# A transformer block with modulated norms: the attention gate wholly on VectorE, its first weights loaded earlier

## The chip, the cores and the metric

One core of one Trainium2 chip runs the whole program. The core has a matmul engine (TensorE, called PE in the profile, with its weight loads as PEld), VectorE (DVE), ScalarE (ACT), GpSimd (POOL) and SyncE (SP), which work on their own instruction queues and wait for each other by semaphores. The metric is the time of one execution on the device in microseconds (us); lower is better. Three executions of the kernel before gave 243.42, 243.48 and 243.65 us, median 243.48.

## The reference

A diffusion-transformer block: batch 2, 256 tokens each, width D = 1152, two heads of 576, MLP width 4608, all in bf16. Six vectors per batch row come from `silu(c) @ w_mod`: shift, scale and gate for attention, and the same three for the MLP.

```python
mod = (silu(c) @ w_mod).reshape(B, 6, 1, D)
shift_a, scale_a, gate_a, shift_m, scale_m, gate_m = [mod[:, i] for i in range(6)]
h = layernorm(x) * (1 + scale_a) + shift_a
q, k, v = split(h @ wqkv)
attn = softmax(einsum('bqhd,bkhd->bhqk', q, k) * Dh ** -0.5)
a = einsum('bhqk,bkhd->bqhd', attn, v).reshape(B, N, D) @ wo
x = x + gate_a * a
h2 = layernorm(x) * (1 + scale_m) + shift_m
return x + gate_m * (gelu(h2 @ w_fc1) @ w_fc2)
```

## The kernel before

All 512 tokens are worked on at once, in 128-row tiles. One big tile in SBUF (`arena`, line 551) is cut by hand into regions, and one in PSUM (`psum`) into eight banks of 512 columns; this is why nearly every row of the profile reads `arena<-psum` or `psum<-arena`, and instructions are told apart by line and shape. All matmuls stand on line 693 (helper `mm`) and all transposes by TensorE on line 696 (`tr`); all loads and stores on line 674 (`dma`); plain evictions out of PSUM on line 688 (ScalarE) or 690 (VectorE), both in `copy_on`.

What sets the order of work: the program is recorded as units (lines 184 to 213) and a planner (`schedule`, line 281) orders them. On PE and SP the order is that of the recording. On VectorE, ScalarE and POOL it is the planner's, by its own cost figures and the length of what hangs on a unit; `order_after` (line 206) adds an edge between two units of one engine, with no data behind it. Each engine then runs its list strictly in order, so one waiting instruction holds all that stand behind it on that engine.

The stages that the change touches, in order of PE:

- K's projection, then `sh` (line 943): the shift of attention by `quad_mm` (line 811). Its stationary operand is the two columns of silu(c), so a matmul makes 2 rows; four of them, at column positions 0, 32, 64 and 96 of the array, take a quarter of the columns each. "A quad" below is such a group of four.
- Q's projection, first six of its nine chunks in one loop over nine input blocks (`q_kt0` to `q_kt8`, line 1202), each as soon as its block of Q's weights has come. SP loads these blocks (`ld_wq0` to `ld_wq8`, line 916), then the weights of the first FG columns of the gate (`ld_ga0`, `ld_ga3`, `ld_ga6`, three blocks each, line 947), V's weights, the rest of the modulation's weights (`ld_modr`), and WO.
- Scores and softmax of four pairs (batch, head) in the order (0,0), (1,0), (0,1), (1,1), by `s_and_softmax` (line 989): VectorE takes the maximum (`smax`, line 1001) and its negative (`snb`, 1002), ScalarE the exponentials (`sexp`, 1005), VectorE the reciprocal (`sri`, 1007) and the normalisation (`spn`, 1009).
- V in twelve tiles of 128 tokens x 384 columns (`v_proj`, line 1023), each evicted by ScalarE, with the four `pt_transposes` (line 1011) of the probabilities between them; their evictions `PT_ev` are VectorE's for batch 0 and ScalarE's for batch 1.
- `rows` (line 1037): more quads, on PE, for the columns of the modulation that VectorE does not make: the rest of the attention gate, and shift and scale of the second norm. Two VectorE transposes (`mt_0`, `mt_1`, line 1046) bring the latter into place.
- `attn_gate` (line 1054): VectorE makes the first FG columns of the attention gate by multiply-add of weight rows with silu(c), in float32, 18 instructions (nine blocks x two batch rows), then 32x32-block transposes, reductions and a small chain over 32 partitions (lines 1067 to 1079). POOL stores the result to a scratch tensor in DRAM; SP loads it back spread over all partitions (`ld_g0`, `ld_g1`, line 1230).
- `pv_halves` and `pv` (attention times V), evicted by `OT_ev`; then `wo_tile` (line 1149): output projection, the product with the gate on VectorE (line 1161), the residual on POOL (1162), and the second norm's statistics.

NG counts the gate's groups of 128 columns that VectorE makes; FG = 128 NG.

Of the kernel before, what the change touches and what calls it, by code (L numbers as in the profile page):

```python
# [493 lines left out]
ALU = mybir.AluOpType  # L494
# [14 lines left out]
F0 = 9  # L509
KC = 5  # L510
KG = 6
NG = 7
FG = NG * 128


# [8 lines left out]
def c_dve_psum32(n):  # L524
    return 110.0 + 1.13 * n


def c_dve_psum16(n):
    return 110.0 + 0.57 * n
# [14 lines left out]
def build_kernel(nc, x, c, wqkv, wo, w_mod, w_fc1, w_fc2, out):  # L544
# [5 lines left out]
    with (  # L550
# [69 lines left out]
        ROWS = sb(O_R + 4 * W1 - 5 * 2304, 2304)[:, 0:288 - 32 * NG]  # L620
# [3 lines left out]
        GBA = sb(O_R + FG * 17, 128)[0:32, :]  # L624
        GTA = sb(O_R + FG * 17 + 128, 128)[0:32, :]
# [51 lines left out]
        def dve(cost, fn, reads, writes, name):  # L677
            return S.op("dve", cost, fn, reads=reads, writes=writes, name=name)
# [7 lines left out]
        def copy_on(eng, dst, src, n, psum16, name):  # L686
            if eng == "act":
                act(c_act(n), lambda e: e.activation(out=dst, in_=src, func=ACTF.Copy), [src], [dst], name)  # L688
            else:
                dve(c_dve_psum16(n) if psum16 else c_dve_psum32(n), lambda e: e.tensor_copy(dst, src), [src], [dst], name)  # L690

        def mm(o, l, r, st, sp, **kw):
            S.instr(lambda e: e.matmul(o, lhsT=l, rhs=r, start=st, stop=sp, **kw), reads=[l, r], writes=[o])  # L693
# [218 lines left out]
                hk(kt, b)  # L912
        k_pair((4, 3), 1, 1)
        k_pair((0, 2, 1, 4, 3), 2, 1)
        for kt in range(KT):
            dma(WQ[:, kt, :], wqkv_v[:, kt, 0:D], P * D * 2, "ld_wq%d" % kt, run=2304)
        for kt in range(KC, KT - 2):
            for b in range(2):
                for i in range(4 - b):
                    k_pair((kt,), i, b)  # L920
# [22 lines left out]
        S.unit("pe", KT * 4 * 31.0 + 100.0, "sh")  # L943
        for kt in range(KT):
            quad_mm(0, WSH[:, kt, :], 0, 9, kt)
        for k0 in range(0, KT, 3):
            dma(WMODR[:, k0:k0 + 3, 0:FG], wmod_v[:, k0:k0 + 3, 2 * D:2 * D + FG], 3 * P * FG * 2, "ld_ga%d" % k0, run=FG * 2)
        dma(WV, wqkv_v[:, :, 2 * D:3 * D], D * D * 2, "ld_wv", run=2304)
        for k0 in range(0, KT, 3):
            dma(WMODR[:, k0:k0 + 3, FG:3 * D], wmod_v[:, k0:k0 + 3, 2 * D + FG:5 * D], 3 * P * (3 * D - FG) * 2, "ld_modr%d" % k0)  # L950
# [38 lines left out]
        def s_and_softmax(b, h):  # L989
            idx = b * 2 + h  # L990
            bank = s_bank[(b, h)]
            S.unit("pe", 8 * c_mm(256), "S_%d_%d" % (b, h))
            ch = head_chunks[h]
            for jq in range(2):
                for ci, (gq, gk) in enumerate(ch):
                    q0 = b * 256 + jq * 128
                    mm(ps32(bank, jq * 256, 256), QK[:, gq, q0:q0 + 128], QK[:, gk, b * 256:(b + 1) * 256], False, ci == len(ch) - 1,
                       skip_group_check=True)
            s3 = ps32(bank).rearrange("p (j k) -> p j k", j=2)
            mx, nb, rsum, ri, pp = MX[:, idx, :], NB[:, idx, :], RS[:, idx, :], RI[:, idx, :], PP[idx]  # L1000
            dve(c_dve_psum32(512), lambda e: e.tensor_reduce(out=mx, in_=s3, axis=AX.X, op=ALU.max), [s3], [mx], "smax_%d" % idx)  # L1001
            dve(165, lambda e: e.tensor_scalar(out=nb, in0=mx, scalar1=-SCALE, scalar2=None, op0=ALU.mult), [mx], [nb], "snb_%d" % idx)  # L1002
            for jq in range(2):
                o, i_, bb, aa = pp[:, jq, :], ps32(bank, jq * 256, 256), nb[:, jq:jq + 1], rsum[:, jq:jq + 1]
                act(c_act(256, 1) + 200, lambda e, o=o, i_=i_, bb=bb, aa=aa: e.activation(out=o, in_=i_, func=ACTF.Exp, scale=SCALE, bias=bb, accum_out=aa),  # L1005
                    [i_, bb], [o, aa], "sexp_%d_%d" % (idx, jq))
            dve(165, lambda e: e.reciprocal(out=ri, in_=rsum), [rsum], [ri], "sri_%d" % idx)
            rib = ri.unsqueeze(2).broadcast_to([P, 2, 256])
            dve(c_dve_tt16(512), lambda e: e.tensor_tensor(out=pp, in0=pp, in1=rib, op=ALU.mult), [pp, ri], [pp], "spn_%d" % idx)

        def pt_transposes(b, h):
            idx = b * 2 + h
# [17 lines left out]
            copy_on("act", V[:, t, ci * CH:(ci + 1) * CH], o, CH, False, "v_ev%d_%d" % (t, ci))  # L1030


        row_parts = ((3, NG, 18), (4, 18, 27))

        last_red = [None]

        def rows():
            S.unit("pe", KT * (864 - 32 * NG) / 2.4 + 500.0, "rows")
            for kt in range(KT):
                for bank, g0, g1 in row_parts:  # L1040
                    quad_mm(bank, WMODR[:, kt, :], g0, g1, kt)
            n = 288 - 32 * NG
            copy_on("act", ROWS, ps32(3, 0, n), n, False, "rows_ev")
            for i, (bank, c0) in enumerate(((3, n), (4, 0))):
                src, dst = ps32(bank, c0, 288), MT[:, i * 288:(i + 1) * 288]
                u = dve(c_dve_psum32(288), lambda e, src=src, dst=dst: e.transpose(dst, src), [src], [dst], "mt_%d" % i)
                S.order_after(u, last_red[0])
            sc, so = MT[:, 288:576].rearrange("p (k r) -> p k r", r=32)[:, :, 0:2], SC1M.rearrange("p (k b) -> p k b", b=2)
            dve(170, lambda e: e.tensor_scalar(out=so, in0=sc, scalar1=1.0, scalar2=None, op0=ALU.add), [sc], [so], "sc1m")
            for b in range(2):  # L1050
                dma(scratch[0, b, FG:D].rearrange("(k q c) -> q k c", q=4, c=32), ROWS[b:128:32, :].rearrange("p (k c) -> p k c", c=32),
                    2304 - 2 * FG, "st_g%d" % b, eng="pool")

        def attn_gate():
            for kt in range(KT):
                for b in range(2):
                    o, w, s1 = ACCA[:, b, :], WMODR[:, kt, 0:FG], ST32[:, b * 9 + kt:b * 9 + kt + 1]
                    if kt == 0:
                        dve(150 + FG * 0.6, lambda e, o=o, w=w, s1=s1: e.tensor_scalar(out=o, in0=w, scalar1=s1, scalar2=None, op0=ALU.mult),  # L1059
                            [w, s1], [o], "ga_%d_%d" % (b, kt))  # L1060
                    else:
                        dve(150 + FG * 1.1, lambda e, o=o, w=w, s1=s1: e.scalar_tensor_tensor(out=o, in0=w, scalar=s1, in1=o, op0=ALU.mult, op1=ALU.add),  # L1062
                            [w, s1, o], [o], "ga_%d_%d" % (b, kt))
            pool(100, lambda e: e.memset(GBA, 0.0), [], [GBA], "gba0")
            for b in range(2):
                a_, t_ = ACCA[:, b, :], ACTA[:, b, :]
                dve(150 + FG * 1.1, lambda e, a_=a_, t_=t_: e.transpose(t_, a_), [a_], [t_], "ga_T%d" % b)
                t3, o = t_.rearrange("p (g r) -> p g r", r=32), GPA[:, 0, b, :]
                last_red[0] = dve(150 + FG * 1.1, lambda e, t3=t3, o=o: e.tensor_reduce(out=o, in_=t3, axis=AX.X, op=ALU.add), [t3], [o], "ga_red%d" % b)
# [7 lines left out]
            g0, gb = GPA[0:32, 0, :, :], GBA.rearrange("p (b g) -> p b g", b=2)[:, :, 0:4 * NG]  # L1077
            dve(200, lambda e: e.tensor_copy(gb, g0), [g0], [gb], "ga_bf")
            dve(200, lambda e: e.transpose(GTA, GBA), [GBA], [GTA], "ga_t")
            for b in range(2):  # L1080
                dma(scratch[0, b, 0:FG].rearrange("(g c) -> g c", c=32), GTA[0:4 * NG, 32 * b:32 * b + 32], FG * 2, "st_ga%d" % b, eng="pool")

        def mlp_gate(prev):
            for b in range(2):
# [31 lines left out]
        def pv_halves():  # L1116
            S.unit("pe", 4 * c_mm(256) + 100.0, "PV_halves")
            for b in range(2):
                for kjt in range(2):
                    for h in range(2):  # L1120
# [110 lines left out]
        v_proj(2, 1)  # L1231
        v_proj(2, 2)
        v_proj(3, 0)
        v_proj(3, 1)
        v_proj(3, 2)
# [108 lines left out]
```

## Time and profile before

| what | value |
|---|---|
| median of three executions | 243.48 us (243.42 to 243.65) |
| the profiled execution's own time | 243.42 us |
| its span, first to last instruction | 241.7 us |
| TensorE matmul busy | 235.7 us (98%) |
| VectorE busy | 115.9 us (48%) |
| ScalarE busy | 68.0 us (28%) |
| GpSimd busy | 21.4 us (9%) |
| bytes moved | 51.58 MB, mean 213 GB/s |

Times in the text are counted from the start of the span. Matmuls overlap in the pipeline, so the time of one in the profile is longer than its share of the stream; what a stage costs is read from the distance between starts, or from the busy time of a stretch. A group line tells line, engine, operation, shapes and count, then busy time and mean duration, then the idle time ahead of it and what ended it. A timeline row starts with its start and its length; consecutive alike instructions are merged into one row with a count. A row of stretches gives, after the stretch, its length and each engine's busy time with the number of instructions (PE, PEld, DVE, ACT, POOL), then the granted clock, the DMA share and GB/s.

### The profile page before, as it was taken

How to read it: one execution, taken by the hardware profiler on the slowest of the kernel's cores; microseconds unless marked ns; L12 is line 12 of the kernel's file. 1: busy time of each engine (PE TensorE's matmuls, PEld its weight loads, DVE VectorE, ACT ScalarE, POOL GpSimd, SP SyncE). 2: the span in 40 equal slices, each digit the busy share in tenths (PEclk: the TensorE clock that was granted, in tenths of full speed). 3: DMA queues.
4: the chain of work that ended last, by engine and by line, in shares of the span. 5: the costliest groups of instructions: out<-in, count | busy, mean ns of one | idle time of the engine just before them, and what ended most of it. 6: DMA issues, size and time to landing. Idle time of an engine off the chain costs nothing.

```text
span 241.7 us, 3956 instructions
## 1 busy us (share of the span) xinstructions
PE 235.7 (98%) x1691; PEld 144.3 (60%) x1699; DVE 115.9 (48%) x229; ACT 68.0 (28%) x137; POOL 21.4 (9%) x38
## 2 busy tenths in 40 slices
PE   6899999999999999999999999999999999999995
PEld 2688844466657666898544444444556666566664
DVE  2654358888994589669999500000122111111112
ACT  4940540546324126973322222333000000000000
POOL 1300000000021476300000110000000000000000
DMA  6999999999994999999963499000000000000000
GB/s 220 369 374 391 390 387 386 404 414 407 391 356 124 321 379 391 392 355 394 343 209 86 122 342 376 8 0 3 0 16 19 16 16 16 19 19 27 22 17 16
DMA packets 30427, 51.58 MB, mean 213 GB/s; under 512 B 1611, under 2 KB 16971, under 8 KB 30411
## 3 DMA queue, kind: packets, MB, share of 16 engines
q1 hardware_dynamic: 29888, 50.73, 58.8%
q0 software_dynamic: 352, 0.60, 0.8%
q8 instruction: 13, 0.21, 0.4%
q10 hardware_dynamic: 171, 0.01, 0.0%
q14 instruction: 3, 0.02, 0.0%
HBM read 50.15 MB, written 1.19 MB: 212 GB/s over the span
## 4 chain that ended last, share of the span: by engine, by line
PE 94%; DMA 3%; SPq 1%; issue 0%; DVE 0%
PE psum L693 92%; DMA arena<-in_wqkv_dram 3%; PE psum L696 2%; SPq L674 1%; DVE arena L1286 0%; DVE arena L1287 0%
## 5 line engine op out<-in xcount | busy, mean ns | idle before, releaser
L693 PE MATMUL psum<-arena 128*128 128x384 bf16 (+9 forms) x1602 | 232.4, 313 | 2.8 <-POOL arena L719 1.5
L693 PEld LDWEIGHTS psum<-arena 128*128 128x128 bf16 (+2 forms) x1610 | 139.0, 97 | 92.0 <-issue 3.8
L1286 DVE TENSOR_TENSOR arena<-psum,arena 128x384 f32<-128x384 f32 (+2 forms) x13 | 6.9, 528 | 88.5 <-PE psum L693 88.5
L1196 ACT ACTIVATE arena<-psum 128x512 bf16<-128x512 f32 (+1 forms) x45 | 22.8, 511 | 42.2 <-PE psum L693 42.2
L688 ACT ACTIVATE arena<-psum 128x512 bf16<-128x512 f32 (+7 forms) x35 | 18.4, 550 | 37.5 <-PE psum L693 37.5
L1091 DVE SCALAR_TENSOR_TENSOR arena<-arena 128x1152 f32<-128x1152 bf16 x16 | 21.3, 1409 | 0.0
L1062 DVE SCALAR_TENSOR_TENSOR arena<-arena 128x896 f32<-128x896 bf16 x16 | 17.7, 1145 | 0.0
L1162 POOL TENSOR_TENSOR arena<-arena 128x384 f32<-128x384 f32 x12 | 10.9, 912 | 13.3 <-DVE arena L1161 11.1
L674 POOL DMA_DIRECT2D dit_scratch<-arena x6 | 3.6, 603 | 92.6 <-ACT arena L688 53.1
L741 DVE BATCH_NORM_STATS2 arena<-arena 128x6 f32<-128x384 f32 (+1 forms) x18 | 9.5, 550 | 4.0 <-DMA arena<-in_x_dram 3.9
L690 DVE CAST arena<-psum 128x512 bf16<-128x512 f32 x11 | 7.5, 690 | 7.4 <-PE psum L693 7.4
L1161 DVE TENSOR_TENSOR arena<-psum,arena 128x384 f32<-128x384 f32 x12 | 6.7, 555 | 3.8 <-PE psum L693 3.8
L1167 ACT ACTIVATE arena<-arena 128x1152 bf16<-128x1152 f32 x4 | 5.4, 1344 | 9.8 <-DVE arena L1166 9.8
L696 PE MATMUL psum<-arena 128*128 128x128 bf16 (+1 forms) x89 | 7.1, 219 | 0.4 <-DMA arena<-in_c_dram 0.4
L696 PEld LDWEIGHTS psum<-arena 128*128 128x128 bf16 (+1 forms) x89 | 5.8, 98 | 2.4 <-DMA arena<-in_c_dram 1.3
L1287 DVE TENSOR_TENSOR arena<-arena 128x384 bf16<-128x384 f32 (+2 forms) x13 | 6.9, 528 | 0.5
L1186 ACT ACTIVATE arena<-psum,arena 128x128 bf16<-128x128 bf16 x16 | 6.1, 455 | 3.0 <-PE psum L696 2.2
L1183 DVE TENSOR_SCALAR arena<-psum,arena 128x128 bf16<-128x128 bf16 x20 | 5.5, 336 | 2.9 <-PE psum L696 2.9
L1005 ACT ACTIVATE arena<-psum,arena 128x256 bf16<-128x256 f32 x8 | 3.7, 469 | 0.4 <-DVE arena L1002 0.3
L745 POOL TENSOR_TENSOR arena<-arena 128x1 f32<-128x1 f32 x6 | 3.3, 553 | 4.5 <-DVE arena L744 4.3
L1001 DVE TENSOR_REDUCE arena<-psum 128x2 f32<-128x512 f32 x4 | 2.7, 686 | 0.9 <-PE psum L693 0.9
L1059 DVE TENSOR_SCALAR arena<-arena 128x896 f32<-128x896 bf16 x2 | 1.3, 684 | 3.6 <-DMA arena<-in_w_mod_dram 3.6
(60 smaller groups left out, 54.1 us busy)
## 6 DMA issues: line engine op xcount, KB each, us to landing
arena<-in_w_fc_dram SPq DMA_DIRECT2D x9, 1152.0 KB, 8.1
arena<-in_w_fc_dram SPq DMA_DIRECT2D x4, 2592.0 KB, 17.5
arena<-in_w_mod_dram SPq DMA_DIRECT2D x3, 1920.0 KB, 19.7
arena<-in_wqkv_dram SPq DMA_DIRECT2D x18, 288.0 KB, 10.0
arena<-in_w_mod_dram SPq DMA_DIRECT2D x3, 864.0 KB, 12.6
arena<-in_wqkv_dram SPq DMA_DIRECT2D x1, 2592.0 KB, 16.9
arena<-in_wo_dram SPq DMA_DIRECT2D x1, 2592.0 KB, 26.1
arena<-in_w_mod_dram SPq DMA_DIRECT2D x1, 2592.0 KB, 18.2
```

What stands on the lines that cost most here:

```text
L688: act(c_act(n), lambda e: e.activation(out=dst, in_=src, func=ACTF.Copy), [src], [dst], name)
L690: dve(c_dve_psum16(n) if psum16 else c_dve_psum32(n), lambda e: e.tensor_copy(dst, src), [src], [dst], name)
L693: S.instr(lambda e: e.matmul(o, lhsT=l, rhs=r, start=st, stop=sp, **kw), reads=[l, r], writes=[o])
L696: S.instr(lambda e: e.transpose(o, i_, idn), reads=[i_, idn], writes=[o])
L741: dve(550, lambda e, s=s, o=o: e.bn_stats(out=o, in_=s), [s], [o], "bn_%s_%d" % (tag, ci))
L1062: dve(150 + FG * 1.1, lambda e, o=o, w=w, s1=s1: e.scalar_tensor_tensor(out=o, in0=w, scalar=s1, in1=o, op0=ALU.mult, op1=ALU.add), [w, s1 ...
L1091: u = dve(1300, lambda e, o=o, w=w, s1=s1: e.scalar_tensor_tensor(out=o, in0=w, scalar=s1, in1=o, op0=ALU.mult, op1=ALU.add), [w, s1, o], ...
L1161: dve(550, lambda e, o=o, ga=ga, x1c=x1c: e.tensor_tensor(out=x1c, in0=o, in1=ga, op=ALU.mult), [o, ga], [x1c], "wo_t1_%d_%d" % (t, ci))
L1162: S.op("pool", 930, lambda e, xs=xs, x1c=x1c: e.tensor_tensor(out=x1c, in0=x1c, in1=xs, op=ALU.add), reads=[x1c, xs], writes=[x1c], name=" ...
L1196: act(c_act(ntok), lambda e: e.activation(out=dst, in_=o, func=ACTF.Gelu_apprx_tanh), [o], [dst], "gelu_%d_%d" % (f, tok0))
L1286: dve(c_dve_psum32(w), lambda e, o=o, gm=gm, t1=t1: e.tensor_tensor(out=t1, in0=o, in1=gm, op=ALU.mult), [o, gm], [t1], "fc2_t1_%d_%d" % ( ...
L1287: dve(c_dve_32(w), lambda e, t1=t1, x1c=x1c, ost=ost: e.tensor_tensor(out=ost, in0=t1, in1=x1c, op=ALU.add), [t1, x1c], [ost], "fc2_out_%d ...
```

## The change

VectorE's share of the attention gate grows from seven groups to all nine (896 to 1152 columns), so no gate column is left to `rows`, and its eviction and two scratch stores fall away. The first of the three gate loads is issued right behind Q's second block of weights. The transposes of the probabilities of (0,1) and (1,1) and the unit `rows` stand later in PE's list. `order_after` edges now put one gate multiply-add behind the normalisation of (0,1) and one behind that of (1,1), the two `mt` transposes behind the end of the gate's small chain, and the eviction `OT_ev_4` behind the second `mt`. The gate's result for both batch rows lies in one transposed tile of 72 groups and is stored in two pieces of 64 and 8 rows.

```diff
-NG = 7
+NG = 9
 FG = NG * 128
...
+        def ga_load(k0):
+            dma(WMODR[:, k0:k0 + 3, 0:FG], wmod_v[:, k0:k0 + 3, 2 * D:2 * D + FG], 3 * P * FG * 2, "ld_ga%d" % k0, run=FG * 2)
+
         for kt in range(KT):
             dma(WQ[:, kt, :], wqkv_v[:, kt, 0:D], P * D * 2, "ld_wq%d" % kt, run=2304)
+            if kt == 1:
+                ga_load(0)
...
-        for k0 in range(0, KT, 3):
-            dma(WMODR[:, k0:k0 + 3, 0:FG], wmod_v[:, k0:k0 + 3, 2 * D:2 * D + FG], 3 * P * FG * 2, "ld_ga%d" % k0, run=FG * 2)
+        for k0 in range(3, KT, 3):
+            ga_load(k0)
...
-            dve(c_dve_tt16(512), lambda e: e.tensor_tensor(out=pp, in0=pp, in1=rib, op=ALU.mult), [pp, ri], [pp], "spn_%d" % idx)
+            u = dve(c_dve_tt16(512), lambda e: e.tensor_tensor(out=pp, in0=pp, in1=rib, op=ALU.mult), [pp, ri], [pp], "spn_%d" % idx)
+            if idx % 2 == 1:
+                S.order_after(ga_units[(1, 7) if idx == 1 else (0, 8)], u)
...
-        row_parts = ((3, NG, 18), (4, 18, 27))
+        row_parts = ((3, 9, 18), (4, 18, 27))
...
-            n = 288 - 32 * NG
-            copy_on("act", ROWS, ps32(3, 0, n), n, False, "rows_ev")
-            for i, (bank, c0) in enumerate(((3, n), (4, 0))):
-                src, dst = ps32(bank, c0, 288), MT[:, i * 288:(i + 1) * 288]
+            for i, bank in enumerate((3, 4)):
+                src, dst = ps32(bank, 0, 288), MT[:, i * 288:(i + 1) * 288]
                 u = dve(c_dve_psum32(288), lambda e, src=src, dst=dst: e.transpose(dst, src), [src], [dst], "mt_%d" % i)
                 S.order_after(u, last_red[0])
+                last_mt[0] = u
...
-            for b in range(2):
-                dma(scratch[0, b, FG:D].rearrange("(k q c) -> q k c", q=4, c=32), ROWS[b:128:32, :].rearrange("p (k c) -> p k c", c=32),
-                    2304 - 2 * FG, "st_g%d" % b, eng="pool")
...
-            dve(200, lambda e: e.transpose(GTA, GBA), [GBA], [GTA], "ga_t")
-            for b in range(2):
-                dma(scratch[0, b, 0:FG].rearrange("(g c) -> g c", c=32), GTA[0:4 * NG, 32 * b:32 * b + 32], FG * 2, "st_ga%d" % b, eng="pool")
+            last_red[0] = dve(200, lambda e: e.transpose(GTA, GBA), [GBA], [GTA], "ga_t")
+            lin = scratch[0].rearrange("b (g c) -> (b g) c", c=32)
+            dma(lin[0:64].rearrange("(j p) c -> p j c", j=2), GTA[:, 0:64].rearrange("p (j c) -> p j c", j=2), 4096, "st_ga0", eng="pool")
+            dma(lin[64:72], GTA[0:8, 64:96], 512, "st_ga1", eng="pool")
...
-            copy_on("dve", OT[:, 4, :], ps32(5), 512, False, "OT_ev_4")
+            S.order_after(copy_on("dve", OT[:, 4, :], ps32(5), 512, False, "OT_ev_4"), last_mt[0])
...
         v_proj(1, 1)
+        v_proj(1, 2)
         pt_transposes(0, 1)
-        v_proj(1, 2)
+        v_proj(2, 0)
+        v_proj(2, 1)
         pt_transposes(1, 1)
-        v_proj(2, 0)
+        v_proj(2, 2)
         rows()
...
-        v_proj(2, 1)
-        v_proj(2, 2)
         v_proj(3, 0)
```

More of the change, by code (lines that the diff above doesn't have):

```diff
@@ L619, in build_kernel @@
         XN2 = [sb(O_R + 4 * W1 - (i + 1) * 2304, 2304) for i in range(4)]
-        ROWS = sb(O_R + 4 * W1 - 5 * 2304, 2304)[:, 0:288 - 32 * NG]
         ACCA = sb(O_R, FG * 8, F32).rearrange("p (b d) -> p b d", b=2)
@@ L623, in build_kernel @@
         GPA = sb(O_R + FG * 16, FG, F32).rearrange("p (q b g) -> p q b g", q=4, b=2)
-        GBA = sb(O_R + FG * 17, 128)[0:32, :]
-        GTA = sb(O_R + FG * 17 + 128, 128)[0:32, :]
+        GBA = sb(O_R + FG * 17, 192)[0:32, :]
+        GTA = sb(O_R + FG * 17 + 192, 192)[0:32, :]
         T1 = [sb(O_X + i * 1536, 1536, F32) for i in range(3)]
@@ L689, in copy_on @@
             else:
-                dve(c_dve_psum16(n) if psum16 else c_dve_psum32(n), lambda e: e.tensor_copy(dst, src), [src], [dst], name)
+                return dve(c_dve_psum16(n) if psum16 else c_dve_psum32(n), lambda e: e.tensor_copy(dst, src), [src], [dst], name)
         def mm(o, l, r, st, sp, **kw):
@@ L1030, in v_proj @@
             copy_on("act", V[:, t, ci * CH:(ci + 1) * CH], o, CH, False, "v_ev%d_%d" % (t, ci))
-        row_parts = ((3, NG, 18), (4, 18, 27))
-        last_red = [None]
+        row_parts = ((3, 9, 18), (4, 18, 27))
+        last_red, last_mt, ga_units = [None], [None], {}
         def rows():
@@ L1061, in attn_gate @@
                     else:
-                        dve(150 + FG * 1.1, lambda e, o=o, w=w, s1=s1: e.scalar_tensor_tensor(out=o, in0=w, scalar=s1, in1=o, op0=ALU.mult, op1=ALU.add),
-                            [w, s1, o], [o], "ga_%d_%d" % (b, kt))
+                        ga_units[(b, kt)] = dve(150 + FG * 1.1, lambda e, o=o, w=w, s1=s1: e.scalar_tensor_tensor(out=o, in0=w, scalar=s1, in1=o,
+                                                                                                               op0=ALU.mult, op1=ALU.add),
+                                                [w, s1, o], [o], "ga_%d_%d" % (b, kt))
             pool(100, lambda e: e.memset(GBA, 0.0), [], [GBA], "gba0")
@@ L1068, in attn_gate @@
                 t3, o = t_.rearrange("p (g r) -> p g r", r=32), GPA[:, 0, b, :]
-                last_red[0] = dve(150 + FG * 1.1, lambda e, t3=t3, o=o: e.tensor_reduce(out=o, in_=t3, axis=AX.X, op=ALU.add), [t3], [o], "ga_red%d" % b)
+                dve(150 + FG * 1.1, lambda e, t3=t3, o=o: e.tensor_reduce(out=o, in_=t3, axis=AX.X, op=ALU.add), [t3], [o], "ga_red%d" % b)
             gp = GPA.rearrange("p q b g -> p q (b g)")
@@ L1076, in attn_gate @@
                 dve(200, lambda e, x_=x_, y_=y_: e.tensor_tensor(out=x_, in0=x_, in1=y_, op=ALU.add), [x_, y_], [x_], "ga_add%d" % b_)
-            g0, gb = GPA[0:32, 0, :, :], GBA.rearrange("p (b g) -> p b g", b=2)[:, :, 0:4 * NG]
+            g0, gb = gp[0:32, 0, :], GBA[:, 0:8 * NG]
             dve(200, lambda e: e.tensor_copy(gb, g0), [g0], [gb], "ga_bf")
-            dve(200, lambda e: e.transpose(GTA, GBA), [GBA], [GTA], "ga_t")
-            for b in range(2):
-                dma(scratch[0, b, 0:FG].rearrange("(g c) -> g c", c=32), GTA[0:4 * NG, 32 * b:32 * b + 32], FG * 2, "st_ga%d" % b, eng="pool")
+            last_red[0] = dve(200, lambda e: e.transpose(GTA, GBA), [GBA], [GTA], "ga_t")
+            lin = scratch[0].rearrange("b (g c) -> (b g) c", c=32)
+            dma(lin[0:64].rearrange("(j p) c -> p j c", j=2), GTA[:, 0:64].rearrange("p (j c) -> p j c", j=2), 4096, "st_ga0", eng="pool")
+            dma(lin[64:72], GTA[0:8, 64:96], 512, "st_ga1", eng="pool")
         def mlp_gate(prev):
```

## The prediction

> **What bounds the kernel now.** I read the page first: its span, the engines' shares and the chain that ended last.
>
> ```profile
> span 241.7 us, 3956 instructions
> ...
> PE 235.7 (98%) x1691; PEld 144.3 (60%) x1699; DVE 115.9 (48%) x229; ACT 68.0 (28%) x137; POOL 21.4 (9%) x38
> ...
> PE 94%; DMA 3%; SPq 1%; issue 0%; DVE 0%
> ```
>
> TensorE (PE) is the chain. Busy shares of pipelined matmuls say little, so I looked next at what PE waited for.
>
> ```profile
> PE psum L693 <- POOL arena L719: 1.5, 1, 1.5
> PE psum L693 <- DMA arena<-in_w_mod_dram: 0.6, 2, 0.4
> PE psum L696 <- DMA arena<-in_c_dram: 0.4, 1, 0.4
> PE psum L693 <- DMA arena<-in_wqkv_dram: 0.2, 1, 0.2
> PE psum L693 <- issue: 0.2, 1, 0.2
> ```
>
> Columns: total us, times, longest. All but the last row lie in the first 11 us, ahead of anything the change touches. After that PE never waits for VectorE (DVE), ScalarE or a load. So the edit can gain only by taking matmul time off PE, and lose only by making PE wait where it does not wait now. The next view is busy time by stretch; the first row is the `rows` unit, the second the shift projection, whose 36 matmuls all have 288 columns.
>
> ```profile
> 64.69:67.14 2.45, 2.45 (x73) 1.62 (x72) 2.45 (x4) 0.49 (x1) 0.00 (x0) 1.00 1.05 384
> 28.68:29.79 1.11, 1.11 (x37) 0.78 (x36) 0.00 (x0) 0.38 (x1) 0.00 (x0) 1.00 1.05 392
> ```
>
> (The 73rd and 37th are a neighbour's tail.) The granted clock is 1.00, so rows can be compared. Four column groups run side by side: 36 matmuls in 1.11 us are 9 passes of 0.122 us. For the edit's longer chains I need VectorE's and ScalarE's rows:
>
> ```profile
> 58.28 0.42 DVE L690 COPY arena<-psum 128x512 bf16<-128x512 bf16 x1 [0.74 <-PE psum L696]
> 62.21 2.21 DVE L1062 SCALAR_TENSOR_TENSOR arena<-arena 128x896 f32<-128x896 bf16 x2
> 72.08 0.23 DVE L1079 STREAM_TRANSPOSE arena<-arena 32x64 bf16<-32x64 bf16 x1
> 106.89 1.54 DVE L1088 TENSOR_SCALAR arena<-arena 128x1152 f32<-128x1152 bf16 x2
> 108.34 21.35 DVE L1091 SCALAR_TENSOR_TENSOR arena<-arena 128x1152 f32<-128x1152 bf16 x16
> 129.72 2.58 DVE L1095 STREAM_TRANSPOSE arena<-arena 128x2304 f32<-128x2304 f32 x1
> ```
>
> ```profile
> 58.06 0.49 ACT L688 ACTIVATE arena<-psum 128x384 bf16<-128x384 f32 x1 [0.73 <-PE psum L693]
> 89.31 1.35 ACT L1167 ACTIVATE arena<-arena 128x1152 bf16<-128x1152 f32 x1 [9.78 <-DVE arena L1166]
> ```
>
> The first line is the eviction that frees the first transposed probabilities; the second the last gate instruction kind at 896 columns; the third the end of the gate at 72.31. The three 1152- and 2304-wide rows belong to the MLP gate and are the very shapes the change needs.
>
> **The change part by part.**
>
> *Rows, removed columns.* Each of 9 passes had a 352-column and a 288-column quad; now two of 288. New unit: 18 x 0.122 = 2.20 us against 2.45, a gain of 0.24 us (the same from the 352 part: 2.45 - 1.11 = 1.34, times 64/352). It is on the chain: PE only. The `rows_ev` eviction on ScalarE (0.22) and two scratch stores on POOL go too, off the chain.
>
> *Moves on PE.* The two transposes go behind one more V tile each, the rows behind V (2,2); as many switches between shapes remain. Zero for PE unless a wait appears.
>
> *First weights ahead of Q's third block.* The two blocks ahead of it land at 29.50 and 30.27. The three shift loads of the same size and shape (864 KB) land 2.3 to 2.55 us apart, so the gate load lands near 32.6 and Q's third block at 33.3 to 33.6 instead of 31.0. PE reaches it after 9 + 12 matmuls of 0.216 us from 30.12, at 34.65. Cover left: 1.1 to 1.35 us. SP issues these loads some 10 us before they land, so its own time (0.5 to 1.1 us for the earlier issue) is hidden. Later loads lag by 3 x 192 KB, 1.5 us: V's weights land at 49.3, first used at 51.7. The three rest-of-modulation loads shrink by as much, so from 62.0 on nothing has moved.
>
> *VectorE's gate.* A 1152-wide multiply-add costs 21.35/16 = 1.33 us where 896 cost 1.06; the first pair 1.54 against 1.28; transposes 1.30 against 1.03 and reductions 1.25 against 1.00 (interpolated between the 896 and 2304 rows). Sum: 16 x 0.27 + 0.26 + 0.54 + 0.5 + 0.1 = 5.7 us more. Starting at 33.7 rather than 37.3, eight of the eighteen fit before Q's evictions at 43.7 (end 43.1), and fourteen instead of thirteen before 58.28. From there follow the built order of both engines. ScalarE now has the eviction of V (0,2), 58.06 above, ahead of the third pair of exponentials, which ran at 56.31; they go to 58.5-59.5. VectorE waits for them: reciprocal 59.6, one multiply-add, normalisation to 61.6-61.7. PE wants that transpose at 62.7 (61.23 + one V tile of 1.46): 1.0 us of cover. The fourth pair ends at 61.2, its normalisation at 63.7, PE wants it at 65.84. Two multiply-adds, transposes and reductions lead to 71.35, the eviction of the second transposed probabilities to 71.7 (needed at 74.4), the small chain (1.69 before, 1.80 in the MLP gate at this width) to 73.5, against 72.31. LN2's two bank transposes (0.81) end at 74.2; the attention evictions start at 76.05: 1.85 us of cover. OT_ev_4, now third in that queue, ends near 78.25; its matmul is due at 79.1.
>
> *The gate's way back.* VectorE's end at 73.5, POOL's issue at 73.8, store landing, SP's issue, load landing. These rows tell of it (count, size, us to landing):
>
> ```profile
> dit_scratch<-arena POOLq DMA_DIRECT2D x2, 0.5 KB, 5.8
> dit_scratch<-arena POOLq DMA_DIRECT2D x2, 1.8 KB, 2.9
> arena<-dit_scratch SPq DMA_DIRECT2D x2, 288.0 KB, 4.3
> ```
>
> The store costs between 2.3 (the MLP gate's, same shape) and 5.95 (the slower of the first pair, issued at 68.0 while weight loads ran); the load between 3.5 and 5.2. I take 2.3 and 3.5, since the weight loads ahead drain at 75.5 as before: gate 0 lands at 79.7, at worst 85.0 (nothing in the rows is quicker). First use is at 80.15. Nor does lateness reach PE at once: the fifth output tile needs the first tile's bank at 84.33, less 0.66; and the first LN2 tile ends on ScalarE at 90.66 (89.31 + 1.35), 1.2 us ahead of its transpose at 91.89, after POOL's five additions of 0.87 that can catch up. Both give 83.7 as the last harmless landing. Loads queued on SP behind the gate move by under 1 us; the next needed one lands at 84.8 for a use past 103.
>
> [...] In the trace the slow pair of stores ran while VectorE was working, the quicker pair while it sat idle (72.31 to 75.36), and after the change two LN2 transposes run right behind the gate. [...]
>
> Sum: the profiled execution took 243.42 us (span 241.7, 1.7 around it); 243.42 - 0.24 + 0 = 243.18. The median of the three runs is 0.06 higher. Forecast 243.2.
>
> **The rivals.**
>
> *Gate rows late (slower).* Place: first output-projection tiles. For it: store rows of 5.95, load rows up to 5.2. Against: the loads that slowed them drain by 75.5. With 5.95 + 3.5 the landing is 83.3, still free; with 5.95 + 5.2 it is 85.0, PE loses 1.3: 244.5. It decides from 83.7.
>
> *A probability transpose that waits.* The third's cover is 1.0 us. If VectorE runs one whole multiply-add (1.33) behind my sum, PE loses 0.3: 243.5; two such, 1.7: 244.9. Against: it is worked out from rows on both sides of the wait.
>
> *Q's third block waits.* Cover 1.1 to 1.35 us; only a landing after 34.65 counts. With another slowest 864 KB spacing (2.55) it would come at 35.9: PE loses 1.2, 244.4. Nothing in the view shows loads out of turn.
>
> *The saving is larger.* If the alternation of two widths also cost something at each of 18 switches, the gain could exceed 0.5 us: under 242.9. Against: 2.45 is already 9 x (0.149 + 0.122).
>
> **How the numbers follow.** What tells from no change is about 0.2%, 0.49 us. Forecast (nothing waits) 0.76, by itself 243.0 to 243.5; late gate 0.06; transpose waits 0.07 (half of it over 0.2%); third block 0.04; larger saving 0.07. Slower: 0.06 + 0.035 + 0.04, so 0.14; faster 0.08 with the scatter; same the remaining 0.78. Range 242.9 to 243.9: it takes in the scatter of the runs (0.23) and the small end of the waits.
>
> **What would show it.** Right: rows stretch 2.2 us; PE's waits unchanged after 11 us; VectorE busy near 121.5; third exponentials at 58.5; gate end near 73.5; gate load issued near 76.2. Wrong: any PE wait on VectorE, ScalarE or a load between 34 and 92, or a gap before the third transpose near 62.7 or before the first LN2 transpose at 91.6.

## The result, and the profile after

The changed kernel takes 242.97 us (median of 22 executions, 242.58 to 244.24) against 243.50 us (22 executions, 243.19 to 243.74) for the kernel before, measured beside it: ratio 0.9979, 95% interval 0.9973 to 0.9986. That is 0.53 us faster, and the interval in microseconds is 0.34 to 0.66. The forecast was a gain of 0.24. So the change does a little more than twice what was forecast, and the question of the experiments is where the other 0.3 us came from.

The first profiled execution of the changed kernel (244.24 us) had TensorE's clock at half for about 3 us of K's projection (granted clock 0.55 from 10.80 to 14.20 us), as one profile of another kernel below (e11) had too (mean granted clock 0.993 in both); so the changed kernel is read below in a second profiled execution, of the unaltered program (e1, 243.08 us). First its page: span and engines' busy time.

```profile
span 241.3 us, 3949 instructions
...
PE 236.2 (98%) x1691; PEld 144.5 (60%) x1699; DVE 121.6 (50%) x229; ACT 67.7 (28%) x136; POOL 20.0 (8%) x36
```

VectorE's busy time is 121.6 us, against 115.9 before and 121.5 forecast. Next what PE waited for in e1 (total us, times, longest).

```profile
PE psum L692 <- POOL arena L718: 1.5, 1, 1.5
PE psum L695 <- DMA arena<-in_c_dram: 0.4, 1, 0.4
PE psum L692 <- DMA arena<-in_wqkv_dram: 0.2, 1, 0.2
PE psum L692 <- issue: 0.2, 1, 0.2
```

No row names VectorE, ScalarE or a load of the gate: every cover that the prediction counted on held. Then the stretch of `rows` in e1 (length, then PE, PEld, DVE, ACT and POOL busy with counts, granted clock, DMA share, GB/s).

```profile
67.90:70.12 2.22, 2.22 (x73) 1.62 (x72) 2.22 (x2) 0.49 (x1) 0.00 (x0) 1.00 1.10 352
```

It was 2.45 and is 2.22. From first start to last start it is 2.331 us before and 2.092 in e1, 0.239 less.

K's projection starts at a moment set by the first loads and differs from execution to execution (10.91 us before, 11.18 in e1), so I compare stretches that begin behind it. From the first transposes of the probabilities (57.86 us in before, 58.14 in e1) to the first matmul of 80 columns (237.42 and 237.46, in the last output tile), PE takes 179.559 us before and 179.320 us in e1: 0.239 less. This is "PE's stretch" below. (Begun in K's projection already, at the five transposes at 15.46 and 15.74 us, the difference is 0.242.) PE gained just what `rows` lost, and nothing was given back. That leaves the stretch behind PE's last matmuls. SyncE's last instructions, before (count, then least, median and longest duration in ns, and first and last start in us):

```profile
L553 SPq COMPARE_BRANCH  x1: 32/32/32, 240.9 to 240.9; - x1
L553 SPq DRAIN  x1: 65/65/65, 241.4 to 241.4; - x1
L553 SPq EVENT_SEMAPHORE  x1: 17/17/17, 241.6 to 241.6; - x1
```

and in e1:

```profile
L553 SPq COMPARE_BRANCH  x1: 33/33/33, 241.0 to 241.0; - x1
L553 SPq DRAIN  x1: 7/7/7, 241.1 to 241.1; - x1
L553 SPq EVENT_SEMAPHORE  x1: 17/17/17, 241.3 to 241.3; - x1
```

Both kernels do the same here: SyncE has waited for the last store, branches out of its list, drains, and ends with a semaphore instruction. From the end of the branch to the start of the drain the trace has 0.410 us before and 0.106 in e1; from the start of the branch to the end of the span 0.715 and 0.353. (Between PE's 80-column matmuls and the branch nothing changed: 3.531 and 3.535 us.) So 0.36 us went out of the last microsecond, far from everything that the change touches on PE and VectorE. The first profiled execution of the changed kernel, with its halved clock ahead, has the same two numbers: PE's stretch 179.320, branch to end 0.357. 0.24 and 0.36 make 0.60, inside the interval of 0.34 to 0.66.

What differs on SyncE is its number of instructions. From its first load to the closing branch it has 77 before and 75 after: two semaphore waits at 75.7 and 76.2 us are gone, those of the gate loads for the two scratch stores of `rows` that the change removed. Of before, by line:

```profile
L471 SPq EVENT_SEMAPHORE  x2: 17/17/17, 75.7 to 76.2; - x2
```

### The profile page after: what moved, and what is told of

Read it like the earlier page. It is cut to its first block, busy times and chain, and to the rows that moved or that the text cites. A ratio compares the mean times of both kernels' runs of the same rounds, so it can differ in the third digit from the quotient of the medians.

```text
span 242.5 us, 3957 instructions
## 1 busy us (share of the span) xinstructions
PE 237.3 (98%) x1699; PEld 145.4 (60%) x1699; DVE 121.5 (50%) x229; ACT 67.8 (28%) x136; POOL 19.9 (8%) x36
## 4 chain that ended last, share of the span: by engine, by line
PE 95%; DMA 3%; SPq 1%; DVE 0%; issue 0%
PE psum L692 93%; DMA arena<-in_wqkv_dram 3%; PE psum L695 2%; SPq L673 1%; DVE arena L1290 0%; DVE arena L1291 0%
## 5 line engine op out<-in xcount | busy, mean ns | idle before, releaser
L692 PE MATMUL psum<-arena 128*128 128x384 bf16 (+8 forms) x1610 | 234.0, 314 | 2.4 <-POOL arena L718 1.5
L687 ACT ACTIVATE arena<-psum 128x512 bf16<-128x512 f32 (+6 forms) x34 | 18.2, 560 | 37.9 <-PE psum L692 37.9
L1064 DVE SCALAR_TENSOR_TENSOR arena<-arena 128x1152 f32<-128x1152 bf16 x16 | 21.9, 1408 | 0.0
L1095 DVE SCALAR_TENSOR_TENSOR arena<-arena 128x1152 f32<-128x1152 bf16 x16 | 21.4, 1414 | 0.0
L673 POOL DMA_DIRECT2D dit_scratch<-arena x4 | 2.4, 609 | 96.6 <-DVE arena L1082 60.3
L695 PEld LDWEIGHTS psum<-arena 128*128 128x128 bf16 (+1 forms) x89 | 6.3, 102 | 2.2 <-DMA arena<-in_c_dram 1.1
L962 ACT ACTIVATE arena<-arena 128x256 bf16<-128x256 bf16 x6 | 2.5, 495 | 1.5 <-DVE arena L956 1.5
```

The costliest lines, as they stand in the source:

```text
L695: S.instr(lambda e: e.transpose(o, i_, idn), reads=[i_, idn], writes=[o])
L1064: ga_units[(b, kt)] = dve(150 + FG * 1.1, lambda e, o=o, w=w, s1=s1: e.scalar_tensor_tensor(out=o, in0=w, scalar=s1, in1=o, op0=ALU.mult, ...
L1095: u = dve(1300, lambda e, o=o, w=w, s1=s1: e.scalar_tensor_tensor(out=o, in0=w, scalar=s1, in1=o, op0=ALU.mult, op1=ALU.add), [w, s1, o], ...
```

## The experiments

Two theories. *PE only*: the gain is the columns taken off `rows`, 0.24 us, and the rest is scatter or luck of the start. *PE and SyncE's end*: 0.24 on PE, and 0.36 because SyncE's list is two instructions shorter. (The recorded expectations call the latter theory A; their theory B seeks the second part in the first 17 us, in loads and clock.) The first four runs were made together, on one chip, where the kernel before took 243.89 us (9 executions, 243.61 to 244.41).

**e1: the changed kernel again.** No edit.

> The changed kernel once more, unaltered, for a trace whose clock is not gated in the first 15 us. Theory A (the matmul rows give 0.24 us, and the way from SyncE's last branch to its drain gives the other 0.3 us, because two waits fewer stand in SyncE's program): the branch-to-drain distance is again 0.1 us where the kernel before has 0.4, and from the first K matmuls of the third token tile on the trace is 0.24 us shorter. Theory B (the other 0.3 us come from the first 17 us, first loads and clock): the branch-to-drain distance varies from run to run and the first K stage ends 0.2 us or more earlier than in the kernel before. Time by both 242.9 to 243.0.

Measured: 243.12 us (243.00 to 243.65), ratio 0.9971 (0.9957 to 0.9985). The gain is there again, and its trace is the one read above.

**e2: the changed kernel with SyncE's list as long as before.** Four waits that have long been satisfied; the program packs two into an instruction, so the list grows by two, to 77.

```diff
             for u in order[e]:
+                if u.name == "ld_wfc1_2":
+                    for _ in range(4):
+                        eng_handle.wait_ge(dma_sems[0], 16)
                 for ins in u.instrs:
```

> The changed kernel with four waits on a load that landed long ago added on SyncE ahead of the third MLP weight load, which makes its program 77 instructions long as in the kernel before (75 in the changed one). Nothing on TensorE moves. Theory A: branch-to-drain back at 0.4 us, time 243.2 to 243.3. Theory B, or a gain that has to do with the gate: no change against the changed kernel, 242.9 to 243.0.

Measured: 243.72 us (243.51 to 243.86), ratio 0.9991 (0.9977 to 1.0004): by the medians 0.17 us faster than before instead of e1's 0.77. SyncE's last instructions in e2:

```profile
L556 SPq COMPARE_BRANCH  x1: 33/33/33, 241.1 to 241.1; - x1
L556 SPq DRAIN  x1: 82/82/82, 241.6 to 241.6; - x1
L556 SPq EVENT_SEMAPHORE  x1: 17/17/17, 241.8 to 241.8; - x1
```

The pause is back, 0.391 us from branch to drain (0.713 from branch to end), and PE's stretch is 179.320 as in e1. The waits stand ahead of an MLP weight load at some 77 us, where SyncE is ahead of need; PE's stretch shows that they cost nothing there, and they cost 0.36 us at 241.

**e3: the kernel before with SyncE's list as short as after.** Four of the closing waits are left out: those for the first four output stores, which land long before the last.

```diff
-                for o in outs[:-1]:
+                for o in outs[4:-1]:
```

> The kernel before without SyncE's closing waits on the four earliest output stores (they land at 177 to 195 us, 45 us and more before the end), so that its program has 75 instructions. All else is unaltered. Theory A: branch-to-drain 0.1 us, time 243.2 (0.3 less than before). Theory B: same as before, 243.5.

Measured: 243.52 us (243.38 to 243.60), ratio 0.9983 (0.9969 to 0.9996), 0.37 us by the medians. PE's stretch is that of before to the nanosecond, 179.559; in e3 the branch is followed by

```profile
L553 SPq COMPARE_BRANCH  x1: 33/33/33, 241.4 to 241.4; - x1
L553 SPq DRAIN  x1: 7/7/7, 241.6 to 241.6; - x1
L553 SPq EVENT_SEMAPHORE  x1: 17/17/17, 241.7 to 241.7; - x1
```

a gap of 0.105 us. So the second gain can be had without the change, and PE's stretch in e2 shows that the change without it keeps the first (e2's time alone, with 1 inside its interval, does not). *PE only* falls. Nor is the pause a matter of the single execution: all seven profiles here with 75 instructions have 0.353 to 0.357 us from branch to end, all three with 77 have 0.712 to 0.715.

**e4: the kernel before with the shorter rows alone.** `row_parts` as in the change, and the quads of bank 3 written where the old ones would leave them; seven groups stay on VectorE and the 64 columns in between, in each of the four quarters, are not made: this kernel leaves out the last 256 columns of the attention gate.

```diff
-        row_parts = ((3, NG, 18), (4, 18, 27))
+        row_parts = ((3, 9, 18), (4, 18, 27))
...
-                    quad_mm(bank, WMODR[:, kt, :], g0, g1, kt)
+                    quad_mm(bank, WMODR[:, kt, :], g0, g1, kt, c0=288 - 32 * NG if bank == 3 else 0)
```

> The kernel before without the 64 gate columns per quarter in the unit rows (two quads of 288 columns per pass; the last 256 columns of the attention gate are then leftovers of the bank, so the output is not the reference's). VectorE, ScalarE, POOL and SyncE programs are unaltered. Theory A and the prediction: rows stretch 2.2 instead of 2.45 us, time 243.26, 0.24 less than before, branch-to-drain still 0.4. If the alternation of two widths cost more than its streams: 243.0 or less.

Measured: 243.89 us (243.53 to 247.49), ratio 0.9994 (0.9981 to 1.0007). The time settles nothing: in the profiled execution K's projection started at 11.84 us, later than in any other profile here (10.81 to 11.42), and one execution of five lies 3.5 us off. The trace does: PE's stretch is 179.320, the 0.24 of the columns and nothing else, and the gap at the end 0.390, as before with its 77 instructions.

**e5, e6, e11: other lengths of SyncE's list.** If the list's length decides, then how? *A shorter list is better*: 76 lies between, 79 and 91 are worse. *A fixed place in the list costs 0.3 us* and moves against the end: it hides wherever SyncE waits anyway. The second took this form after e5 and e6, and e11 was run to test it. The edit is e2's, with 2, 32 and 8 waits.

> The changed kernel with SyncE's program at 76 instructions (one more than its 75, one fewer than 77). Theory A so far knows 75 (0.11 us from branch to drain) and 77 (0.39 to 0.41). If the distance depends on where the end of the program falls against a boundary of what has been fetched, 76 gives one of the two values and nothing between; if it grows with each instruction, 0.25. TensorE's stretch from the third transposes to the last block stays at 179.32 us.

> The same with 91 instructions on SyncE (16 more than the changed kernel). A boundary that recurs would give 0.11 us again at some length, a distance that only grows more than 0.4, a single threshold 0.4. TensorE's stretch unchanged at 179.32 us.

> The changed kernel with SyncE's program at 79 instructions. With 75, 76 and 77 the pause of about 0.3 us stood behind the last instruction, between the drain and the last semaphore, and between the branch and the drain: it moves back by one instruction as one is added. At 79 it should lie ahead of the branch, where SyncE waits for the last store to land anyway: branch to end 0.35 us as with 75, and the time of the changed kernel, 0.5 us under the kernel before. If the pause only depends on the length being 77 or more: 0.71 us.

Measured: e5 242.99 us, ratio 0.9978 (0.9965 to 0.9991); e6 243.08, 0.9983 (0.9972 to 0.9994), both beside 243.47 for the kernel before; e11 243.06, 0.9972 (0.9956 to 0.9988), beside 243.70. Their intervals overlap; the times alone do not rank them. The traces do (us, worked out from the starts and ends of SyncE's last instructions):

```
instructions   branch end to   drain start to   branch start to
               drain start     last semaphore   end of span
75 (e1)        0.106           0.152            0.353
76 (e5)        0.108           0.428            0.586
77 (e2)        0.391           0.226            0.713
77 (before)    0.410           0.210            0.715
79 (e11)       0.129           0.152            0.381
91 (e6)        0.128           0.152            0.382
```

With 76 the pause stands one instruction further back, between the drain and the last semaphore, as its lines show:

```profile
L556 SPq COMPARE_BRANCH  x1: 33/33/33, 241.0 to 241.0; - x1
L556 SPq DRAIN  x1: 7/7/7, 241.1 to 241.1; - x1
L556 SPq EVENT_SEMAPHORE  x1: 17/17/17, 241.5 to 241.5; - x1
```

With 79 and 91 it is nowhere behind the branch. Counted from the first load, the place lies between SyncE's 77th instruction and its 78th. With 79 the 78th is the wait for the last store, where SyncE stands still for 0.6 us in any case; with 91 it is the issue of an output store at 211 us, for which SyncE has waited since 206. So it is no matter of shorter or longer: one place in SyncE's instruction stream costs some 0.3 us, and 76 and 77 are the lengths that put it behind the last store, between two instructions that end the program. With 75 the count puts it behind the last instruction.

What is at that place, the DMA rows of the pages show. They list queues of the kind "instruction"; these are the rows of queue q14 inside the span (packets, MB, share), first of e1, then of e6:

```profile
q14 instruction: 3, 0.02, 0.0%
q14 instruction: 4, 0.03, 0.0%
```

The fourth packet, of 8 KB, is there in the trace of each of the thirteen profiles, most often behind the span, and its start follows the list. With 91 instructions it starts at 206.81 us, 1.03 us behind the end of the 77th; with 79 at 242.88, again 1.03 behind it; with 77 and 75 it comes after the end of the span, 0.98 to 1.07 behind the 77th (in before 241.98, in e1 242.36), with 76 1.33 behind. So at every length of the list the packet starts 0.98 to 1.33 us behind the 77th instruction. That the next instructions are fetched there, and that the pause is the price of starting this fetch, is the author's reading and not shown. It is no wait for the bytes, since with 77 instructions the packet starts 0.6 us after SyncE has gone on. At the end of this program the place takes 0.28 to 0.30 us: 0.428 less 0.152 with 76 instructions, 0.391 and 0.410 less 0.106 with 77.

**e7: the old places on PE.** The changed kernel with V tiles, probability transposes and `rows` in the old order.

```diff
         v_proj(1, 1)
-        v_proj(1, 2)
         pt_transposes(0, 1)
-        v_proj(2, 0)
-        v_proj(2, 1)
+        v_proj(1, 2)
         pt_transposes(1, 1)
-        v_proj(2, 2)
+        v_proj(2, 0)
         rows()
...
+        v_proj(2, 1)
+        v_proj(2, 2)
         v_proj(3, 0)
```

> The changed kernel with TensorE's old order of V tiles, transposes and rows; all else as changed. From my sum of VectorE's and ScalarE's queues the normalisations of (0,1) and (1,1) end at 61.7 and 63.65 (in the kernel before's times), while the old order wants the transposes at 61.23 and 63.3: TensorE waits 0.45 and 0.3 us on VectorE, stretch 180.05 us instead of 179.32, time about 243.7. If the later places are not needed: no wait, 179.32, 243.0.

Measured: 243.65 us (243.49 to 245.10), ratio 1.0014 (0.9995 to 1.0032). PE's stretch is 180.040, 0.72 longer than in e1. PE waits for the normalisation ahead of both transposes, here the third's row of the waits:

```profile
PE psum L695 <- DVE arena L1013: 0.2, 1, 0.2
```

That row holds only part of it. From one group's first start to the next group's, V (1,1) takes 1.865 us instead of 1.462, and V (1,2) 1.760: 0.40 and 0.30. VectorE ends the two normalisations at 61.92 and 63.92; the old order wants them at 61.6 and 63.3. The later places are what keeps the longer multiply-adds free.

**e8: the first gate load at its old place.** The changed kernel, with all three gate loads behind Q's blocks.

```diff
-            if kt == 1:
-                ga_load(0)
...
-        for k0 in range(3, KT, 3):
+        for k0 in range(0, KT, 3):
             ga_load(k0)
```

> The changed kernel with the first gate load back behind all of Q's blocks. VectorE then starts its 18 instructions at 37.9 instead of 33.7 and does 5 instead of 8 before Q's evictions: three 1.33 us instructions more later on. My sum: the second transposed probabilities are evicted at 75.3 (wanted 74.4, TensorE waits 1.0 us), the LN2 transposes end at 79.4 (banks 3 and 4 wanted at 77.7, 1.7 us): stretch 182.0, time 245.6, between 244.9 and 246.2. If VectorE has slack enough without the early load: 179.32 and 243.0.

Measured: 245.19 us (244.92 to 245.36), ratio 1.0065 (1.0042 to 1.0088); PE's stretch 181.483, 2.16 longer than in e1. PE's new waits:

```profile
PE psum L692 <- DVE arena L1048: 1.2, 1, 1.2
PE psum L692 <- DVE arena L689: 0.5, 1, 0.5
```

VectorE's reductions for the gate now end 3.7 us later: the second eviction of probabilities runs at 75.16 instead of 71.47, where `pv_halves` wants it at 74.8 (that unit takes 1.370 us instead of 0.560), and the `mt` transposes end at 79.6 instead of 74.4, which holds the evictions queued behind them (PV takes 4.856 instead of 3.504). 0.81 and 1.35 make the 2.16. I expected 2.7; the place is right, the size 0.5 high.

**e9, e10: a late gate.** The prediction says that lateness of the first gate load reaches PE only from a threshold on. Six and ten additions of 128x384 on GpSimd, on a region that is free at that time, hold back the store.

```diff
             last_red[0] = dve(200, lambda e: e.transpose(GTA, GBA), [GBA], [GTA], "ga_t")
+            prev = None
+            for i in range(6):
+                x_, y_ = ACTA[:, 0, 0:384], ACTA[:, 1, 0:384]
+                prev = S.op("pool", 1, lambda e, x_=x_, y_=y_: e.tensor_tensor(out=x_, in0=x_, in1=y_, op=ALU.add), ...)
...
+            late = dma(lin[0:64]..., eng="pool")
+            S.order_after(late, prev)
```

> The changed kernel with six additions of 128 x 384 float32 on POOL, on the gate's scratch space after it has been used, ahead of the gate's first store: only the gate's way back is late. POOL starts them at the end of the reductions (71.5 on VectorE's list) and needs 0.87 us each, so the store is issued at about 76.9 instead of 74.0 and the first gate lands near 82.3 instead of 79.4. My prediction puts the last harmless landing at 83.7 (84.0 in a run whose K stage starts 0.3 us later): no wait on TensorE, stretch from the third transposes to the last block 179.32 us, although the first product with the gate waits 1.9 us. If the gate's landing is on the chain: 1.9 us longer.

> The same with ten additions: store issued near 80.4, gate landing near 85.8. By my rule TensorE loses 85.8 less 84.0, 1.8 us (1.4 to 2.4), at the fifth output tile or at the first LN2 transpose: stretch 181.1 us. If the gate's lateness passes on in full: 6.4 us less the 1.0 us that it has today. If it never reaches TensorE: 179.32.

Measured: e9 244.07 us (243.65 to 244.62), ratio 1.0012 (0.9995 to 1.0029); e10 250.54 (249.82 to 251.27), ratio 1.0284 (1.0243 to 1.0325). Both are dearer than expected, so I looked for the place. In e9, PE waits for the `mt` transposes, and VectorE waits for the gate (timeline rows: start, length; the bracket is idle time ahead and what ended it):

```profile
PE psum L692 <- DVE arena L1050: 0.7, 1, 0.7
```

```profile
72.39 1.89 DVE L1076 COPY arena<-arena 32x72 f32<-32x72 f32 x3
74.31 2.23 DVE L1079 TENSOR_TENSOR arena<-arena 32x72 f32<-32x72 f32 x3
76.58 1.01 DVE L1081 CAST arena<-arena 32x72 bf16<-32x72 f32 x1
...
83.83 1.02 DVE L1171 TENSOR_TENSOR arena<-psum,arena 128x384 f32<-128x384 f32 x2 [2.17 <-DMA arena<-dit_scratch]
```

Against e1:

```profile
71.91 0.62 DVE L1076 COPY arena<-arena 32x72 f32<-32x72 f32 x3
72.56 0.62 DVE L1079 TENSOR_TENSOR arena<-arena 32x72 f32<-32x72 f32 x3
73.22 0.18 DVE L1081 CAST arena<-arena 32x72 bf16<-32x72 f32 x1
73.44 0.27 DVE L1082 STREAM_TRANSPOSE arena<-arena 32x96 bf16<-32x96 bf16 x1
73.64 0.79 DVE L1050 STREAM_TRANSPOSE arena<-psum 128x288 f32<-128x288 f32 x2
...
76.35 0.69 DVE L689 CAST arena<-psum 128x512 bf16<-128x512 f32 x1 [1.91 <-PE psum L692]
```

The additions waited for the reductions alone and ran from 72.11 on, beside VectorE's small chain, which took 5.2 us instead of 1.5; with it went the `mt` transposes and the evictions behind them. That is where e9's 1.05 us on PE lie: PV takes 4.555 us instead of 3.504. The additions disturbed another wait than the one they were made for. The late gate itself cost e9 nothing: it landed at 83.74, VectorE idled 2.17 us for it, and the nine output tiles from 80.299 on still took 13.163 us (13.162 in e1). By the prediction's rule the last harmless landing is the start of the fifth tile less 0.66, 80.30 + 4 x 1.4625 - 0.66 = 85.5 here, so this run only says that 1.75 us short of it nothing is lost.

e10 crosses it. Its gate landed at 89.77, and the waits have

```profile
PE psum L692 <- DVE arena L1171: 4.3, 1, 4.3
```

The landing was 4 us later than I had worked out: the ten additions took 1.07 us apiece from start to start, where I had counted 0.87, so that the store was issued at 82.73, and store and load then took 3.44 and 3.59. The prediction's rule, from the start of the output tiles at 80.175, gives 85.4, so 4.4 us of waiting; measured 4.3. But the tiles took 19.941 us, 6.78 more. The rest is TensorE's clock, in stretches of e10 (columns as above; the granted clock is third from the end):

```profile
86.20:88.00 1.80, 0.00 (x0) 0.00 (x0) 0.00 (x0) 0.00 (x0) 0.00 (x0) 1.00 0.36 78
88.00:89.00 1.00, 0.00 (x0) 0.00 (x0) 0.00 (x0) 0.00 (x0) 0.00 (x0) 0.70 0.96 233
89.00:90.47 1.47, 0.00 (x0) 0.00 (x1) 0.61 (x2) 0.00 (x0) 0.00 (x0) 0.50 0.90 261
...
94.50:95.00 0.50, 0.50 (x3) 0.22 (x2) 0.50 (x3) 0.00 (x0) 0.20 (x1) 0.50 1.09 350
95.00:95.50 0.50, 0.50 (x4) 0.27 (x3) 0.25 (x1) 0.00 (x0) 0.50 (x1) 0.78 1.08 344
95.50:96.00 0.50, 0.50 (x5) 0.30 (x4) 0.07 (x1) 0.00 (x0) 0.50 (x2) 1.00 1.14 359
```

The clock falls to half 2.2 us into the wait and comes back at 95.2, 4.7 us after PE has work again: 2.4 us of work lost. 4.3 + 2.4 is 6.7 of the 6.78. (Half the clock over 4.7 us makes the 2.4; it is worked out, not measured apart.) This is one profiled execution; what sets the 2.2 us and the 4.7 us it does not show.

No version tried is faster than the changed kernel beyond the noise: the intervals of e5, e6 and e11 overlap with its own.

## Why the prediction was right or wrong

- *Rows*: forecast a gain of 0.24; measured 0.239 in `rows` (2.331 to 2.092) and 0.239 over all of PE. The nine passes of 0.122 us were the right row to count by.
- *Moves on PE*: forecast zero, and zero it was. e7 gives the price of leaving them out, 0.72 us. The third exponentials started at 58.73 (forecast 58.5), the normalisation ended at 61.86 and PE took its transpose at 62.97: 1.1 us of cover, 1.0 forecast.
- *First weights early*: the gate load landed at 32.66 (forecast 32.6), Q's third block at 33.43 (33.3 to 33.6), V's weights at 49.73 (49.3). No wait of PE. e8 gives the price of the old place, 2.16 us.
- *VectorE's gate*: `ga_t` ended at 73.71, forecast 73.5; with K's projection 0.27 later in e1 the forecast would be 73.7. LN2's transposes ended at 74.43, and VectorE then idled 1.91 us for PE; 1.85 were forecast.
- *The gate's way back*: the store issued at 74.01 landed in 1.98 us (2.3 taken from the MLP gate's row), the load in 3.45 (3.5), gate 0 at 79.45 (79.7 forecast). The prediction notes that two LN2 transposes run behind the gate, and that the slow pair of stores ran while VectorE was working. With these transposes running (0.79 us for the two) the store took 1.98 us, its neighbour 1.56, nowhere near the slow row of 5.95. They read PSUM, and in e9 they took 0.43 us each beside one of GpSimd's additions, as in e1; VectorE's copies and additions within SBUF took 1.89 and 2.23 us for three beside GpSimd's additions there, instead of 0.62 each time.
- *Around the span*: this is the step that failed. The prediction says of the removed parts that "two scratch stores on POOL go too, off the chain", and takes the rest of the execution as it was ("1.7 around it" the span, and the same end of the span). Of those stores it counts POOL's side and not the waits for them on SyncE, and it passes over the "SPq 1%" in its own line of the chain. That term was set to zero and measured 0.36 us (0.715 to 0.353 from the closing branch to the end). A zero would have been a fair guess for two waits that cost nothing where they stand; what I did not ask is whether the pause of 0.41 us between SyncE's branch and its drain, in plain sight in the trace of before, depends on how many instructions stand ahead of it.
- *The rivals*: none of the three waits came. "The saving is larger" came out nearest in sign, but by another mechanism: the switches between widths cost nothing, since PE's gain is the 0.239 us of the columns and no more, with the change and in e4.

The median of 242.97 lies within the range of 242.9 to 243.9, near its low end. That is luck in part: the low end allowed for the scatter of the runs (0.23), not for a gain at the end of the program, and the prediction's sum with the 0.36 taken off, 243.18 - 0.36 = 242.82, lies below the range. The chances did not follow the cause: with 0.24 + 0.36 the gain is just over what these measurements tell from no change, and that case had 0.08.

## What to carry to other kernels

Count what an edit removes on every queue, waits included, and read the last microsecond of the trace as its own stage: the distance from the last store's landing to the end of the span changed by 0.36 us with the number of instructions on SyncE (from the closing branch 0.353 us with 75, 0.713 and 0.715 with 77). When a gain is larger than the stage it was meant for can give, compare stretches that begin and end on the same instructions; here they split 0.24 on PE from 0.36 at the end, which the total times alone could not. And a delay that is added to test one wait must not slow other work that PE waits for, or it tests another: beside e9's additions VectorE's small chain took 5.2 us instead of 1.5.

## What the runs showed of the hardware that was not expected

- A pause of some 0.3 us sat at a fixed place of SyncE's instruction stream, behind the 77th instruction from the first load, and an 8 KB packet of the kind "instruction" started 0.98 to 1.33 us behind that instruction: the pause stood behind the closing branch with 77 instructions, behind the drain with 76, and nowhere behind the branch with 79 and 91, where the 78th stands at a wait anyway (0.713, 0.586, 0.381 and 0.382 us from branch to end).
- GpSimd additions of 128x384 in float32 held up small VectorE instructions of 32x72 although these are narrow: in e9 three VectorE copies took 1.89 us instead of 0.62, three additions 2.23 instead of 0.62, a cast 1.01 instead of 0.18. Five of the seven took 0.76 to 1.04 us, and each of the five ended 0.05 to 0.09 us after one of GpSimd's additions had ended; the other two, which began together with an addition, took 0.19 and 0.22, as in e1, and these two additions are e9's longest, 1.05 and 1.08 us. The other four took 1.00, as did the one in e10 that ran with VectorE idle, so GpSimd lost little. What causes this is not shown.
- TensorE's clock was halved with no long wait ahead: in the changed kernel's first profile it was 0.55 from 10.80 to 14.20 us, in K's projection, which follows a group of matmuls of two columns. The longest wait of PE in the 9 us before was 0.53 us; in e10 the clock fell 2.2 us into a wait.

```profile
10.81 3.31 PE L692 MATMUL psum<-arena 128*128 128x256 bf16 x16 [0.16 <-DMA arena<-in_wqkv_dram]
```

The same 16 matmuls took 1.92 us in the profile of before. It differs between executions: e1, the same program, has a clock of 1.00 there. What starts it was not looked into.
